# A gated attention and token-mixing kernel: the first loads of x, wv and gate_w issued in another way, and all engines' orders written anew

## The chip, the core and the metric

The kernel runs on one core of one Trainium2 chip. The core has five engines that run at the same time: PE (TensorE, matrix products into PSUM), DVE (VectorE), ACT (ScalarE), POOL (GpSimd) and SP (SyncE, which here only issues DMAs). Sixteen DMA engines move data between HBM and the on-chip memory SBUF; SP and ACT each have a queue for them. The metric is the device time of one execution in microseconds (us), as the median of several runs.

## The reference

x has 2048 rows (tokens) of 448 columns, all in bf16. Two branches are computed from it and mixed by a gate.

```python
g = sigmoid((x * gate_w).sum(-1, keepdims=True))          # one gate per row
a = A(x, wq, wk, wv, wo, beta)
b = B(x, w1, b1, w2, b2)
out = g * a + (1 - g) * b

# A: 16 heads of 28; four segments of 512 rows
q, k, v = x @ wq, x @ wk, x @ wv                          # split into heads and segments
p = softmax(q_s @ k_s.T * 28**-0.5 + mask)                # mask: only keys up to the query, within the segment
a_mem = (phi(q_s) @ M) / (phi(q_s) @ z + 1e-6)            # phi(t) = t + 1 for t > 0, else exp(t)
o_s = sigmoid(beta) * a_mem + (1 - sigmoid(beta)) * (p @ v_s)
M, z = M + phi(k_s).T @ v_s, z + sum(phi(k_s))            # memory of the segments before
A = o @ wo

# B: mixes over the tokens
h = layernorm(x)
u = gelu(h.T @ w1 + b1)                                   # 448 x 1792
B = (u @ w2 + b2).T
```

## The kernel before

**Tiles.** x is held twice: `xh` has 16 tiles of 128 rows (it becomes the layer-normed h in place), and `xT` has the same data transposed, as four overlapping pieces of 128 columns (`C0`) by 2048 rows, in four chunks `tc` of 512 rows. For chunk 0, PE transposes the tiles x0 to x3 with the identity matrix (`trx0_0`, `trx0_1` from x0 and x1, `trx1_0`, `trx1_1` from x2 and x3), and ACT or DVE copies each result from PSUM to `xT` (`xTcp0_00` and so on, lines 695 and 697; the last two digits are the half and the pair of pieces). The other chunks are loaded by transposing DMAs (`dtx1_0` to `dtx3_1`, line 535).

**Projections.** `project` (L711) makes q, k and v: two products of 64 contraction rows each run side by side in the array, so that one step is a pair. `v03` is v of the tiles 0 to 3, with one more column that holds gate_w and gives the gate's sum; `k0`, `q0` are k and q of chunk 0; `k1`, `q1`, `v67` belong to chunk 1. A projection is split into parts: a and b (the first four steps of two outputs each), c and d (the last three). Only `v03` is cut further: `v03s` and `v03t` are the first two steps of a and b, which need two of the three pieces of wv alone (`R_wv[0:2]`), so that they can start before the last piece. The results leave PSUM by `cpv`, `cpk`, `cpq` on ACT or DVE; `gt` takes the tanh of the gate's column on ACT. wk and wq are re-arranged to groups of 32 columns by `padk`, `padx`, `padq` (L655). gate_w comes as rows to `gstage`; PE transposes it (`gtr`) and DVE writes it as the last column of wv (`gw`).

**Attention.** The work has 16 units (4 segments by 4 groups of 4 heads), in 8 pairs. A pair has five steps: `sc` (scores on PE, L973, into the PSUM banks 0 to 3), `exp` (ACT, L982, 128 x 2048) and `mask` (POOL, L985). Each `sc` writes the same four banks, so it waits for the `exp` before it. `pv` is the product with v; `ta`, `rec`, `oa`, `ot` and others finish a unit on DVE. `ek`, `mk`, `phk`, `tk` make phi(k), `mst` and `mem` the memory term. `wo` is the output projection and `ag` its gated evacuation.

**Token mixing.** `bns`, `bna`, `vpe`, `rstd`, `ln` are the layer norm (DVE and POOL). `u` (224 products) and `y` (224, the last tile in two parts) are the two layers on PE; `gsq`, `gvh`, `garg`, `gth`, `gelu` are the gelu on ACT and DVE, `fin` mixes the branches, `out` stores. w1 and w2 come in 15 pieces through three slots (`ldw1_0` to `ldw2_7`). The biases come by `ldb1` and `ldb2`; `btr` on PE turns them into columns.

**Order.** Each engine runs its operations strictly in the order of a list written out in `ORDER` (L308): the names above, with the PSUM banks after "=", and "u1-0:2" for two in a row. An operation that ACT or DVE (or DVE or POOL) can do runs on the engine in whose list it stands. `Sched.plan` reads the lists and `finalize` places a semaphore wait wherever an operation needs another engine's result. An engine that waits holds up everything behind it in its list. The list of SP is the order of its DMA issues.

At the start SP issues x0, then x2 and x3 as one piece, then wv in three pieces, wk and wq in two each; ACT issues x1 and the two pieces of gate_w. POOL makes the identity matrix (`id0`, `id1`, L594 and L595) and clears what must be zero (`z3_0`, `z3_1`, L607, and `v0`, `v1`, L611). PE fills its time with products of no use (`warm`, `fill0` to `fill5`, L640) until x has landed.

Of the kernel before, what the change touches and what calls it, by code (L numbers as in the profile page):

```python
# [5 lines left out]
ACT = mybir.ActivationFunctionType  # L6
# [6 lines left out]
D = 448  # L13
# [288 lines left out]
def pool_cost(n):  # L302
# [7 lines left out]
        warm fill0 fill1 trx0_1=4 trx0_0=5 trx1_1=6 fill2 fill3 gtr fill4 trx1_0=7 fill5 v03s v03a v03t v03b v03c v03d  # L310
        k0a=54 k0b=67 k0c k0d q0a q0b q0d q0c v67a=54 sc0_0 k1a=67 v67c k1c sc0_1 k1b=45 k1d sc0_2 q1a=76 q1b=45 q1c
        q1d sc0_3 u1-0:2=7 u0-0:2=6 u1-2 pv0=4 u1-3 u0-2:3 sc0_4 u0-5:2 u1-4 u0-7 btr=4 u3-0=5 u1-5:3 u3-1 u0-8 u3-2
        u2-0=4 sc1_0 u1-8 u0-9:2 u2-1 u1-9 u2-2:3 u1-10 u2-5:2 u1-11 u0-11 sc1_1 u2-7 u3-3 u0-12 u1-12 u3-4 u1-13:2
        u0-13:2 u2-8 u1-15 u3-5:2 u0-15 u2-9 sc1_2 u2-10 u3-7:3 u4-0:2=7 u2-11:2 u4-2 pv1=6 sc1_3 u3-10 u2-13 u3-11
        u4-3 u5-0:2=6 u4-4 u2-14 u5-2:2 u3-12 u4-5:2 u2-15 u5-4 sc1_4 u3-13:2 u4-7 u5-5 u4-8 u5-6 u7-0=4 u3-15 u5-7
        u7-1:2 u5-8 u4-9 sc2_0 u7-3 u5-9 u4-10 u5-10 u4-11 u5-11:2 u6-0=5 u4-12:3 u6-1 u7-4 u6-2 u4-15 u6-3 sc2_1
        u5-13 u7-5 u6-4 u7-6:3 u5-14:2 pv2=7 sc2_2 u6-5:3 u7-9 u6-8 mst0=7 u7-10 u6-9 pv3=6 u6-10 sc2_3 u7-11:2 u8-0=7
        u7-13:2 u9-0=6 u6-11 u7-15 u8-1:5 u9-1 sc2_4 u6-12 u9-2 u6-13:2 u8-6 u9-3:2 u8-7 u9-5 u6-15 mem4=4 u8-8 u9-6
        u8-9 u9-7:2 sc3_0 u9-9:2 u8-10 pv4=4 u9-11 u8-11 u9-12 u8-12 u9-13 u8-13 u9-14 u8-14 u9-15 u8-15 k2a=54 sc3_1
        k2c k2b=67 k2d sc3_2 q2a=54 q2b=67 q2c q2d sc3_3 v96a=45 v96b=67 v96c v96d sc3_4 u10-0:4=4 pv5=7 u10-4:3  # L320
        mem5=6 mem6=5 u11-0:5=7 sc4_0 u10-7 u11-5:3 u10-8 u11-8 u10-9:2 pv6=5 sc4_1 u13-0=6 u10-11 u11-9:2 u12-0=5
        u10-12 u12-1 u10-13:3 u12-2:3 u11-11 u13-1 u12-5 u11-12:3 u13-2 u11-15 u12-6:2 sc4_2 u12-8 u13-3:3 pv7=4
        mst1=7 u12-9:2 sc4_3 u13-6:2 mem7=7 wo2=4 u13-8 u12-11 u13-9 u12-12 sc4_4 wo0~2=7 u12-13:2 u13-10:4 u12-15
        wo3=4 u13-14:2 wo1=7 sc5_0 k3a=45 k3b=76 k3c k3d sc5_1 v14a=45 pv8=7 v14c pv9=6 wo5=7 mem9=5 sc5_2 q3a=46
        q3b=75 q3c q3d sc5_3 mem8=4 y1-0:2=6 y0-0:2=7 y1-2:2 y3-0:4=4 y1-4:2 sc5_4 y3-4 y0-2:2 y1-6 y0-4 y3-5 y1-7
        y3-6 y0-5 y1-8 y3-7 y1-9:2 sc6_0 y3-8 y0-6 y3-9 y1-11 y0-7 y3-10 y0-8:2 wo4=5 y1-12 sc6_1 y0-10:3 y1-13 wo6=5
        y3-11:3 y0-13 sc6_2 mem11=6 pv10=5 mst2=4 mem10=7 pv11=6 sc6_3 y5-0=5 y2-0=4 y5-1 y2-1 y5-2:2 y2-2 y5-4:2
        y4-0=7 y5-6:2 y4-1:3 sc6_4 y4-4 y6-0=6 y5-8 y6-1 y5-9 y4-5 y2-3 y4-6 y2-4 y4-7 y5-10 y6-2 y4-8 sc7_0 y5-11
        y4-9 y6-3 y4-10:3 y2-5 y4-13 y6-4 y5-12 y2-6 y5-13 y6-5:2 sc7_1 y2-7 wo7=7 y2-8:4 y7-0:2=5 y2-12 y6-7 y2-13
        sc7_2 mem12=7 y7-2:2 pv12=4 y7-4:3 y6-8 mem13=7 sc7_3 y7-7:2 y6-9 y7-9:2 y6-10 y7-11 y6-11:3 wo10=4 y7-12  # L330
        mem14=7 sc7_4 y7-13 pv13=4 wo11=6 wo9=5 wo8=4 y8-0:2=7 y9-0=6 pv14=5 y9-1 pv15=4 y9-2 y8-2 y9-3 y8-3 mem15=5
        y9-4:2 y8-4 y9-6:2 y8-5:3 y9-8 y8-8 y9-9 y11-0:3=5 y9-10 y11-3 y9-11 y11-4 y9-12:2 y10-0=4 y8-9:3 y10-1 y11-5
        y8-12:2 y10-2 y11-6 y10-3 y11-7 y10-4 y11-8 y10-5 y11-9 y10-6:2 y11-10 y10-8 y11-11:2 wo13=6 y10-9:2 wo15=7
        wo14=6 y11-13 wo12=7 y10-11 y13-0:3=6 y15-0:2=5 y14-0=7 y15-2 y14-1 y10-12 y13-3 y15-3:2 y14-2:2 y10-13 y13-4
        y14-4 y15-5 y14-5 y13-5 y15-6 y12-0=4 y14-6 y15-7 y14-7 y13-6 y12-1 y13-7 y14-8:2 y15-8 y12-2 y13-8 y14-10:3
        y15-9 y13-9 y15-10 y12-3 y13-10 y15-11 y12-4:2 y14-13 y13-11:2 y15-12:2 y12-6 y13-13 y12-7:7 y15-0~2=7 y15-1~2
        y15-2~2 y15-3~2 y15-4~2 y15-5~2 y15-6~2 y15-7~2 y15-8~2 y15-9~2 y15-10~2 y15-11~2 y15-12~2 y15-13~2
    """,
    "ACT": """
        ldx1 ldgwb ldgw xTcp0_11 cpv2 gt2 cpv0 cpv1 gt1 gt3 gt0 cpk0_0 ek0_0 cpk0_2 cpk0_3 cpq0_3 cpq0_2 gt4 cpq0_1  # L340
        ek0_1 exp0_0=2 cpv6 gt7 gt6 exp0_1=3 cpk1_3 cpk1_2 exp0_2=4 ek0_2 cpq1_0 cpq1_1 exp0_3=0 cpv5 tb gt5 exp0_4=1
        eq1_1 eq1_0 exp1_0=5 exp1_1=6 eq1_2 gsq1 gsq0 exp1_2=2 ek0_3 gth0 ek1_0 exp1_3=3 gth1 gsq2 exp1_4=0 gth2 gsq3
        exp2_0=1 ek1_1 gth3 gsq4 exp2_1=4 gsq5 gvh5 exp2_2=5 gth5 exp2_3=6 gth4 gsq7 exp2_4=0 gsq6 gth7 ek1_3 exp3_0=2
        gth6 eq1_3 gsq9 gsq8 ek1_2 exp3_1=3 cpk2_1 cpk2_3 cpq2_3 exp3_2=1 cpq2_1 cpv8 gt8 exp3_3=4 cpv9 gt9 cpv11 gt12
        gt11 gt10 exp3_4=7 eq2_1 gth9 ek2_1 exp4_0=0 eq2_0 gth8 exp4_1=5 gsq10 eq2_2 gvh10 ek2_0 gsq11 exp4_2=6 gth10
        exp4_3=2 gth11 ag2 exp4_4=3 gsq12 ag3 gsq13 gvh13 exp5_0=1 cpk3_0 cpk3_3 exp5_1=4 cpv15 gth13 gt15 gt14 eq2_3
        ag5 gth12 exp5_2=7 cpq3_0 ek2_3 exp5_3=0 ek2_2 eq3_2 exp5_4=5 eq3_0 eq3_1 gt13 exp6_0=2 ag4 exp6_1=3 exp6_2=6
        exp6_3=1 exp6_4=4 exp7_0=0 exp7_1=5 ag7 exp7_2=7 eq3_3 exp7_3=2 ag10 exp7_4=3 ag11 ag9 ag8 ag14 ag12
    """,
    "DVE": """  # L350
        xTcp0_00 xTcp0_01 gw bns2 xTcp0_10 bns0 bns1 padk1 bna1 padk0 bns3 bna2 padq0 padq1 bna0 padq3 bna3 padq2 ob0
        cpv3 ln2 ln0 cpk0_1 mk0_0 phk0_0 ln1 bns4 cpv4 bna4 cpq0_0 bns5 bns7 bns6 bna5 bns8 bna6 cpv7 bna7 bns11 bns15
        mk0_1 cpk1_1 cpk1_0 bns9 cpq1_3 bna11 bna15 mo0 bns10 ln4 bna10 ln3 ln5 bns13 ln6 cpq1_2 bna8 ln7 mk0_2 bna9
        bna13 bns12 ta0 bns14 ln9 ln8 bna14 bna12 omgh ln10 rec0 b2c b1c b1h gh mg0 ln11 mq1_0 oc0 phk0_2 mo1 ln12
        ln14 phk0_1 ln13 oc1 oc2 oc3 ln15 mg1 oa0 b1s gvh1 gvh0 phq1_0 garg0 mo2 ta1 gelu0 mk0_3 mg2 gcol0 rec1 garg1
        phk0_3 omg0 b2g0 gelu1 gvh2 mk1_0 garg2 mq1_1 gcol1 phk1_0 gvh3 gelu2 garg3 phq1_1 mo3 gelu3 gvh4 oa1 omg1 ta2
        rec2 mk1_1 garg5 mg3 mq1_2 garg4 msta0 ta3 ot1 gelu5 phk1_1 rec3 ot0 gvh7 mstc0 gelu4 garg7 tm4 oa2 gvh6 garg6
        gelu7 ta4 mk1_3 gelu6 phq1_2 gvh9 gvh8 oa3 garg9 eps4 cpk2_0 rec4 cpk2_2 ot2 phk1_3 mq1_3 om4 mk1_2 cpq2_0
        cpq2_2 phk1_2 garg8 oa4 cpv10 cpv12 ot3 ta5 phq1_3 tm6 tm5 mk2_1 eps6 gelu9 eps5 phk2_1 mq2_1 rec5 ta6 oa5
        gelu8 om5 mq2_0 rec6 ot4 oa6 garg10 gvh11 phq2_0 msta1 ta7 phq2_1 garg11 tm7 mq2_2 mstc1 eps7 gelu10 om6 b2g1  # L360
        gelu11 ag0 ot5 gvh12 rec7 ag1 om7 oa7 garg13 ot6 cpk3_1 cpk3_2 cpq3_3 mk2_0 ot7 ta8 cpv14 ta9 garg12 tm9
        phk2_0 gelu13 gelu12 cpq3_1 cpq3_2 tm8 mk2_3 eps8 phk2_3 mq2_3 rec8 om8 phq2_3 eps9 mk2_2 mq3_2 phk2_2 cpv13
        rec9 om9 mq3_1 gcol2 phq2_2 oa9 omg2 oa8 fin1 ag6 fin3 fin0 tm11 ta10 msta2 tm10 eps11 ta11 eps10 mq3_0 rec11
        b2g2 phq3_2 gcol3 rec10 phq3_1 om10 oa11 ot8 om11 oa10 phq3_0 ot9 fin4 fin5 ot10 mstc2 fin2 tm12 ta12 eps12
        tm13 ot11 rec12 mq3_3 om12 oa12 phq3_3 fin6 fin7 ta13 eps13 tm14 rec13 ot12 oa13 eps14 om13 ta14 rec14 tm15
        ta15 om14 oa14 eps15 ot13 rec15 om15 omg3 oa15 ot14 fin9 b2g3 ot15 fin8 ag13 ag15 fin11 fin10 fin14 fin15
        fin13 fin12 fin15~2
    """,
    "POOL": """
        mhalf v0 id0 z3_1 id1 z3_0 padx1 v1 padx0 vpe0 rstd0 maskg0 vpe4 mask0_0_0 mask0_1_1 rstd4 mask0_1_3 mask0_2_2  # L370
        mask0_2_2~2 vpe8 rstd8 vpe12 rstd12 mask0_4_1 mask1_1_1 mask1_0_0 mask0_4_3 mask0_3_0 wo0 mask1_2_2 mask1_4_1
        mask1_2_2~2 mask2_0_0 mask1_1_3 mask1_3_0 mask2_1_1 mask1_4_3 mask2_2_2 mask2_2_2~2 mask2_3_0 mask2_1_3
        mask3_1_1 mask3_0_0 mask2_4_1 mask3_2_2 mask2_4_3 o4 mask3_3_0 mask3_1_3 mask3_4_1 mask3_2_2~2 o5 mask3_4_3
# [17 lines left out]
def build_kernel(nc, X, WQ, WK, WV, WO, BETA, W1, B1, W2, B2, GW, OUT):  # L391
    NSL, NP = 3, 5
    sch = Sched(nc, {"psum": (4, 5, 6, 7), "p": tuple(range(NP))}, {"p": {}})
    op = sch.op
# [43 lines left out]
    wvx = sb([128, NCT, D + 4])  # L438
# [812 lines left out]
```

## Time and profile before

| | us |
|---|---|
| median of 13 runs | 174.52 (173.71 to 175.99) |
| profiled execution, its own time | 174.22 |
| its span, first to last instruction | 172.5 |
| PE busy (share of the span) | 167.5 (97%) |
| DVE busy | 146.1 (85%) |
| ACT busy | 126.4 (73%) |
| POOL busy | 68.9 (40%) |

The profile is of one execution; its own time is its span and 1.72 us around it. Rows of the profile are groups or merged stretches of instructions: line of the code, engine, operation, what is written and read (all SBUF and PSUM tiles are called t), how often, busy time, and in brackets the idle time before and what ended it. PEld is the weight load that comes before each product. Products are pipelined and their ends are modelled, so that a PE that reads as fully busy need not run at its peak.

### The profile page before, as it was taken

The page shows a single profiled execution, that of the slowest core. Times are in us where ns is not written, and L with a number is a line of the kernel's source. Part 1 is how long each engine was busy: PE and PEld are TensorE (multiplying, and loading weights), DVE is VectorE, ACT ScalarE, POOL GpSimd, SP SyncE. Part 2 cuts the span into 40 slices and gives each one's busy share as a digit, 9 for nine tenths or more (in the row PEclk, how much of TensorE's full clock was granted, in tenths as well). Part 3 has the DMA queues.
Part 4 walks back from the last instruction along what each step waited for, and adds up shares of the span by engine and source line. Part 5 has one row for each costly group of instructions (what it writes and reads, how often), then busy time and mean ns, then how long its engine had stood idle before and what let it go on. Part 6 is the DMA issues. An engine that isn't in the chain of part 4 may idle for free.

```text
span 172.5 us, 4631 instructions
## 1 busy us (share of the span) xinstructions
PE 167.5 (97%) x1900; PEld 81.2 (47%) x1900; DVE 146.1 (85%) x326; ACT 126.4 (73%) x151; POOL 68.9 (40%) x99
## 2 busy tenths in 40 slices
PE   7999999999999999999999999999999999999994
PEld 3444344444445443445554434444644445554552
DVE  0899999879887999998989999998999699885123
ACT  2168999799998999999999989997757876003000
POOL 6250184352355300554270581456428765320000
PEclk9999999999999999999999999999999999999999
DMA  5999999248379459523159340150911878027103
GB/s 151 279 200 274 285 250 257 74 103 241 66 209 145 77 119 307 151 60 72 38 144 292 112 130 0 32 70 12 272 63 55 218 209 260 12 82 211 39 18 106
DMA packets 49749, 24.57 MB, mean 142 GB/s; under 512 B 14256, under 2 KB 49488, under 8 KB 49728
## 3 DMA queue, kind: packets, MB, share of 16 engines
q1 hardware_dynamic: 49576, 24.16, 55.4%
q8 instruction: 15, 0.25, 0.6%
q10 hardware_dynamic: 152, 0.12, 0.2%
q14 instruction: 6, 0.05, 0.1%
HBM read 18.76 MB, written 2.36 MB: 122 GB/s over the span
## 4 chain that ended last, share of the span: by engine, by line
PE 81%; DVE 13%; DMA 3%; SPq 1%; issue 1%
PE t L284 44%; PE t L711 13%; PE t L286 13%; PE t L973 6%; PE t L1011 5%; DMA t<-in_A_wv_dram 3%; DVE t L916 2%; DVE t L749 1%; DVE t L1048 1%; PE t L858 1%; DVE t L761 1%; DVE t L1071 1%; DVE t L1027 1%; DVE t L832 1%; DVE t L1040 1%
## 5 line engine op out<-in xcount | busy, mean ns | idle before, releaser
L284 PE MATMUL t<-t 128*128 128x448 bf16 (+2 forms) x431 | 83.0, 347 | 0.0
L982 ACT ACTIVATE t<-t 128x2048 bf16<-128x2048 f32 x40 | 75.0, 1876 | 8.7 <-PE t L973 8.4
L985 POOL TENSOR_SCALAR_AFFINE_SELECT t<-t 128x512 bf16<-128x512 bf16 x64 | 42.8, 689 | 47.5 <-ACT t L982 46.9
L284 PEld LDWEIGHTS t<-t 128*128 128x128 bf16 x431 | 39.6, 98 | 38.6 <-issue 4.8
L711 PE MATMUL t<-t 64*128 64x512 bf16 (+1 forms) x308 | 35.1, 368 | 1.0 <-DMA t<-in_A_wv_dram 0.4
L286 PE MATMUL t<-t 128*32 128x448 bf16 (+1 forms) x428 | 24.7, 356 | 0.3 <-DVE t L1027 0.2
L1042 POOL TENSOR_TENSOR t<-t 128x448 bf16<-128x448 f32 x12 | 15.5, 1293 | 21.6 <-DVE t L1038 10.3
L711 PEld LDWEIGHTS t<-t 64*128 64x128 bf16 x308 | 15.7, 94 | 17.6 <-PE t L711 1.9
L1118 DVE SCALAR_TENSOR_TENSOR t<-t 128x448 bf16<-128x448 f32 (+2 forms) x17 | 10.7, 645 | 10.1 <-PE t L284 9.9
L1067 ACT ACTIVATE t<-t 128x448 bf16<-128x448 f32 x11 | 7.8, 722 | 14.5 <-PE t L284 14.4
L973 PE MATMUL t<-t 28*128 28x512 bf16 (+3 forms) x256 | 15.8, 301 | 0.1
L286 PEld LDWEIGHTS t<-t 128*32 128x32 bf16 x428 | 10.2, 96 | 8.7 <-issue 2.2
L1027 DVE STREAM_TRANSPOSE t<-t 128x512 f32<-128x512 f32 x16 | 11.3, 705 | 1.9 <-PE t L1011 1.8
L1011 PE MATMUL t<-t 128*32 128x256 bf16 (+3 forms) x256 | 11.9, 300 | 0.3 <-issue 0.3
L973 PEld LDWEIGHTS t<-t 28*128 28x128 bf16 x256 | 4.5, 92 | 14.4 <-issue 4.7
L1048 DVE STREAM_TRANSPOSE t<-t 128x512 bf16<-128x512 bf16 x16 | 11.0, 688 | 0.0
L916 DVE BATCH_NORM_STATS2 t<-t 128x6 f32<-128x448 bf16 x16 | 9.4, 609 | 0.0
L1011 PEld LDWEIGHTS t<-t 128*32 128x32 bf16 x256 | 6.7, 96 | 5.9 <-issue 2.0
L1100 DVE SCALAR_TENSOR_TENSOR t<-t 128x448 bf16<-128x448 f32 x14 | 8.9, 645 | 0.4 <-ACT t L1098 0.4
L1025 DVE STREAM_TRANSPOSE t<-t 128x512 f32<-128x512 f32 x12 | 8.4, 707 | 0.8 <-PE t L284 0.6
L1095 DVE SCALAR_TENSOR_TENSOR t<-t 128x448 f32<-128x448 f32 x14 | 8.9, 636 | 0.0
L1087 ACT ACTIVATE t<-t 128x448 f32<-128x448 f32 x14 | 8.7, 638 | 0.2
(73 smaller groups left out, 165.2 us busy)
## 6 DMA issues: line engine op xcount, KB each, us to landing
t<-in_B_w_dram SPq DMA_DIRECT2D x7, 1024.0 KB, 6.3
t<-in_B_w_dram SPq DMA_DIRECT2D x8, 896.0 KB, 5.3
out_dram<-t SPq DMA_DIRECT2D x15, 112.0 KB, 3.6
t<-in_A_x_dram SPq DMA_DIRECT2D x3, 448.0 KB, 4.6
t<-in_A_wo_dram SPq DMA_DIRECT2D x4, 98.0 KB
t<-in_A_wk_dram SPq DMA_DIRECT2D x1, 336.0 KB, 4.5
t<-in_A_wq_dram SPq DMA_DIRECT2D x1, 336.0 KB, 4.8
spare_heads<-t SPq DMA_DIRECT2D x8, 32.0 KB
```

Of the source, the lines that this page charges most:

```text
L284: return e.matmul(out, w, x, skip_group_check=True, **kw)
L286: last = e.matmul(out[q : q + 32], w[:, q : q + 32], x, skip_group_check=True, **kw)
L711: last = e.matmul(bank(o["b"])[:, 0 : o["n"]], o["w"](r, c), o["x"](r, c), start=first, stop=end, skip_group_check=True)
L916: op("DVE", lambda e: e.bn_stats(st6[:, t, :], xh[:, t, :]), reads=[R_x[t]], writes=[R_st6[t]], name=f"bns{t}", cost=512, prio=P_PROJ - 10)
L973: last = e.matmul(bank(hl)[:, c0 : c0 + w], kT[r, hg, s * 512 + j * 128 : s * 512 + j * 128 + 128], qT[r, hg, s * 512 + 128 * j : s * 512 ...
L982: op("ACT", lambda e: e.activation(pslot(g), ps[:, 0:4, :], ACT.Exp, scale=SCALE), reads=R_bank[0:4], writes=[g.res], take=g, name=f"exp{p ...
L985: op("POOL", lambda e, c0=c0: e.affine_select(pslot(g)[:, :, c0 : c0 + 128], pslot(g)[:, :, c0 : c0 + 128], pattern=[[0, 4], [1, 128]], co ...
L1011: last = e.matmul(bank(cb)[32 * hl : 32 * hl + 32, 128 * j : 512], vaug[:, 4 * s + j, 32 * h : 32 * h + 32], pslot(P_fill[u // 2][f])[:, h ...
L1027: dv(lambda e: e.transpose(t2[:, 0, :], bank(cb)[:, 0:512]), [bres(cb)], [R_tt[tb][0]], "ta", 630, use=(cb,))
L1042: op("POOL", lambda e: e.tensor_tensor(o3, n3[0], n3[1], op=ALU.add), reads=R_tt[tb], writes=[R_ob[tb]], name=f"o{u}", cost=1280, port=Tru ...
L1048: dv(lambda e: e.transpose(oT[:, hg, s * 512 : s * 512 + 512], o), [R_ob[tb]], qres(hg, s), "ot", 635)
L1118: op("DVE", lambda e: e.scalar_tensor_tensor(outst[:, p, c0:c1], bank(b)[:, 0 : c1 - c0], omg[:, T : T + 1], ag(T)[:, c0:c1], op0=ALU.mult ...
```

## The change

Three things are edited.

- The loads. x0 and x1 come as one DMA on SP, x2 and x3 as one on ACT (224 KB each). The first piece of wv (the last 128 rows, 112 KB) stays on SP, and the other two become one DMA of 336 KB on ACT that fills both `R_wv[1]` and `R_wv[2]`. The two pieces of gate_w move from ACT to SP, behind the first piece of wv.
- The lists of all five engines are new. They hold the same operations apart from the loads. Seventeen go to ACT from DVE (xTcp0_00, xTcp0_10, cpv3, cpk0_1, cpk1_1, cpq1_3, gvh1, gvh7, gvh9, cpk2_0, cpq3_3, cpv13, cpv14, ag0, ag1, ag6, ag13), ten from ACT to DVE (cpv0, cpv6, cpk0_2, cpk1_2, gvh5, cpk2_1, gvh10, gvh13, cpv15, ag4), and three from DVE to POOL (padk1, padq2, padq3).
- On SP the load of x4 to x7 comes before the transposing loads of chunk 1, `dtx2_0` takes the early place of `dtx2_1`, and `ldb1` goes behind `ldw1_1`.

The loads, and the heads of the lists:

```diff
-    load_x("SP", 0, 1)
-    load_x("ACT", 1, 1)
-    op("ACT", lambda e: e.dma_start(gstage[0:3, :], GW[0:384].rearrange("(c p) -> c p", p=128)),
+    load_x("SP", 0, 2)
+    load_x("ACT", 2, 2)
+    op("SP", lambda e: e.dma_start(gstage[0:3, :], GW[0:384].rearrange("(c p) -> c p", p=128)),
        writes=[R_gst[0]], name="ldgw", dma=True, prio=-3, cost=450, nbytes=2000)
-    op("ACT", lambda e: e.dma_start(gstage[3:4, :], GW[320:448].rearrange("(c p) -> c p", p=128)),
+    op("SP", lambda e: e.dma_start(gstage[3:4, :], GW[320:448].rearrange("(c p) -> c p", p=128)),
        writes=[R_gst[1]], name="ldgwb", dma=True, prio=-3, cost=450, nbytes=2000)
     op("SP", lambda e: e.dma_start(wvx[:, 3, 0:D], WV[320:448]), writes=[R_wv[0]], name="ldwv0", dma=True, prio=-3,
        cost=450, nbytes=114688)
-    for k, c, n in ((1, 0, 1), (2, 1, 2)):
-        op("SP", lambda e, c=c, n=n: e.dma_start(wvx[:, c : c + n, 0:D],
-                                                 WV[128 * c : 128 * (c + n)].rearrange("(c p) d -> p c d", p=128)),
-           writes=[R_wv[k]], name=f"ldwv{k}", dma=True, prio=-3, cost=450, nbytes=114688 * n)
-    load_x("SP", 2, 2)
+    op("ACT", lambda e: e.dma_start(wvx[:, 0:3, 0:D], WV[0:384].rearrange("(c p) d -> p c d", p=128)),
+       writes=R_wv[1:], name="ldwv1", dma=True, prio=-3, cost=450, nbytes=344064)
...
     "PE": """
-        warm fill0 fill1 trx0_1=4 trx0_0=5 trx1_1=6 fill2 fill3 gtr fill4 trx1_0=7 fill5 v03s v03a v03t v03b v03c v03d
-        k0a=54 k0b=67 k0c k0d q0a q0b q0d q0c v67a=54 sc0_0 k1a=67 v67c k1c sc0_1 k1b=45 k1d sc0_2 q1a=76 q1b=45 q1c
+        warm fill0 trx0_1=4 fill1 trx0_0=5 trx1_1=6 fill2 trx1_0=7 fill3 gtr fill4 fill5 v03t v03s v03a v03b v03c v03d
+        k0a=46 k0b=57 k0c k0d q0b q0a q0d q0c v67a=46 sc0_0 v67c k1a=57 k1c sc0_1 k1b=64 k1d q1a=75 sc0_2 q1c q1b=64
...
     "ACT": """
-        ldx1 ldgwb ldgw xTcp0_11 cpv2 gt2 cpv0 cpv1 gt1 gt3 gt0 cpk0_0 ek0_0 cpk0_2 cpk0_3 cpq0_3 cpq0_2 gt4 cpq0_1
-        ek0_1 exp0_0=2 cpv6 gt7 gt6 exp0_1=3 cpk1_3 cpk1_2 exp0_2=4 ek0_2 cpq1_0 cpq1_1 exp0_3=0 cpv5 tb gt5 exp0_4=1
-        eq1_1 eq1_0 exp1_0=5 exp1_1=6 eq1_2 gsq1 gsq0 exp1_2=2 ek0_3 gth0 ek1_0 exp1_3=3 gth1 gsq2 exp1_4=0 gth2 gsq3
+        ldx2 ldwv1 xTcp0_11 xTcp0_00 xTcp0_10 cpv3 cpv2 gt3 cpv1 gt2 gt0 cpk0_0 gt1 ek0_0 cpk0_1 ek0_1 cpk0_3 cpq0_2
+        gt4 cpq0_1 cpq0_3 exp0_0=2 gt7 gt6 tb cpk1_1 exp0_1=3 cpk1_3 cpq1_3 exp0_2=4 cpq1_0 cpq1_1 exp0_3=0 cpv5 gt5
+        ek0_2 exp0_4=1 eq1_2 exp1_0=5 eq1_1 eq1_0 exp1_1=6 gsq0 gsq1 gvh1 exp1_2=2 gth0 ek0_3 gth1 exp1_3=3 eq1_3 gsq2
...
     "DVE": """
-        xTcp0_00 xTcp0_01 gw bns2 xTcp0_10 bns0 bns1 padk1 bna1 padk0 bns3 bna2 padq0 padq1 bna0 padq3 bna3 padq2 ob0
-        cpv3 ln2 ln0 cpk0_1 mk0_0 phk0_0 ln1 bns4 cpv4 bna4 cpq0_0 bns5 bns7 bns6 bna5 bns8 bna6 cpv7 bna7 bns11 bns15
+        bns0 bns2 xTcp0_01 bna0 gw bns1 bns3 padk0 bna1 bna2 padq1 bna3 padq0 bns6 bns5 cpv0 bns7 bns4 ln0 ln3 bna4
+        mk0_0 bna7 phk0_0 cpk0_2 cpv4 bna6 cpq0_0 bns13 bna5 bns8 bns11 cpv7 cpv6 bns10 bna8 omgh cpk1_0 bns9 ln4 ln1
...
     "POOL": """
-        mhalf v0 id0 z3_1 id1 z3_0 padx1 v1 padx0 vpe0 rstd0 maskg0 vpe4 mask0_0_0 mask0_1_1 rstd4 mask0_1_3 mask0_2_2
+        z3_1 v0 z3_0 id0 v1 id1 padx0 padk1 padx1 vpe0 mhalf padq2 rstd0 padq3 wo0 maskg0 vpe4 mask0_0_0 rstd4
...
     "SP": """
-        ldx0 ldx2 ldwv0 ldwv1 ldwv2 ldwk0 ldwk=0 ldwq0 ldwq=1 ldbeta ldb2 dtx1_0 dtx1_1 ldx4 ldx12 ldb1 ldx8 dtx2_1
-        tk0_0 ldw1_0 ldw1_1 gk0_2 gk0_1 gk0_3 ldw1_2 gq0_2 gq0_1 gq0_0 gk0_0 gq0_3 gk0_h1 gk0_h0 gq0_h1 gq0_h2 gq0_h0
+        ldx0 ldwv0 ldgw ldgwb ldwk=0 ldwk0 ldwq=1 ldwq0 ldx4 dtx1_0 ldbeta dtx1_1 ldx8 ldx12 dtx2_0 tk0_0 ldw1_0 ldb2
+        ldw1_1 ldb1 gk0_1 gk0_3 gk0_2 ldw1_2 gq0_0 gq0_1 gq0_2 gq0_3 ldwo2 gk0_0 gq0_h2 gq0_h1 gk0_h1 gk0_h0 gq0_h0
...
```

## The prediction

> **What bounds the kernel now.** I read the busy time by stretch first (columns: stretch, its length, busy time and count of PE, weight loads, DVE, ACT, POOL, the granted clock, DMA share, GB/s).
>
> ```profile
> 0.00:7.07 7.07, 5.74 (x33) 2.90 (x34) 2.19 (x6) 1.88 (x2) 2.98 (x10) 1.00 0.73 199
> 16.69:30.00 13.31, 12.96 (x155) 5.64 (x156) 13.22 (x42) 12.98 (x17) 6.27 (x10) 1.00 1.03 257
> 30.00:60.00 30.00, 29.69 (x373) 14.14 (x372) 25.98 (x69) 27.75 (x31) 13.32 (x20) 1.00 0.58 132
> 60.00:90.00 30.00, 29.80 (x464) 14.24 (x461) 28.50 (x57) 29.54 (x40) 10.71 (x15) 1.00 0.49 122
> 90.00:120.00 30.00, 29.76 (x273) 13.42 (x269) 29.17 (x60) 27.79 (x33) 14.28 (x18) 1.00 0.42 100
> 120.00:146.00 26.00, 26.00 (x389) 13.21 (x384) 24.33 (x49) 18.84 (x14) 14.79 (x21) 1.00 0.60 171
> ```
>
> After 7.07 PE is never free for long: what delays its first product delays the end, unless a later stall shrinks. But ACT is nearly full too from 16.7 to 120 us (98.06 of 103.31), and DVE from 16.7 to 30. Next the chain of waits: its shares, then its pieces in order (start, length, what).
>
> ```profile
> PE 81%; DVE 13%; DMA 3%; SPq 1%; issue 1%
> ...
> 2.71 4.32 DMA t<-in_A_wv_dram
> 7.07 7.23 PE t L711 x66
> ```
>
> The last piece of wv lands at 2.71 + 4.32 = 7.03 and opens the dense stretch. The timeline has the other steps of the head:
>
> ```profile
> 2.42 0.30 POOL L595 TENSOR_SCALAR_AFFINE_SELECT t<-t 128x128 bf16<-128x128 bf16 x1
> 3.58 1.20 PEld L683 LDWEIGHTS t<-t 128*128 128x128 bf16 x12 [0.50 <-DMA t<-in_A_x_dram]
> 5.09 0.60 ACT L695 ACTIVATE t<-t 128x512 bf16<-128x512 bf16 x1 [1.71 <-PE t L683]
> 9.57 0.54 ACT L830 ACTIVATE t<-t 128x448 bf16<-128x448 f32 x1 [3.89 <-PE t L711]
> 16.69 0.40 PE L973 MATMUL t<-t 28*128 28x512 bf16 x4
> ```
>
> Identity ready at 2.72, first transposes at 3.58 when x has landed, the ACT copy at 5.09, the first evacuation of v at 9.57, the first scores (sc0_0) at 16.69. Of the waits, in us, times, longest:
>
> ```profile
> POOL t L985 <- ACT t L982: 46.9, 20, 9.8
> ACT t L982 <- PE t L973: 8.4, 11, 1.4
> PEld t L973 <- ACT t L982: 4.6, 13, 0.5
> ```
>
> Each scores step needs the exp before it to have left banks 0 to 3, so PE and ACT march together. Transfers of x take this from issue to landing:
>
> ```profile
> DMA to landing us min/median/max: 2.5/2.7/2.8
> ```
>
> **What the skill says.** "DMA: Bandwidth & Descriptors", section "Issuing engines are not separate DMA queues": DMAs of SP and ACT run on the same 16 engines; a second issuer saves only issue time. The trace agrees so far: two 112 KB pieces on two queues landed together at 3.3 and 3.5. "TensorE: Matmul & The Clock Gate", Part 1: a free-running window of about 3.4 us decides whether the array runs at half clock. Here 512-column warm-up products start 0.42 us apart, later ones 0.21, though the granted clock reads 1.00 throughout. "GPSIMD Engine Reference", section 4.1: one-input operations run at roughly line rate; its 3.1 measures about 2.6 cycles an element for two-input ones. The 512-element select in this trace takes 0.64 us, 1.25 ns an element.
>
> **The head, part by part.** Names are mapped to rows in order (each engine has as many rows as its list has names).
>
> x: the four tiles go out at 0.80 and 0.81 as two 224 KB pieces. Before, all 448 KB had landed at 1.26 + 2.8 = 4.06, the first two tiles at 3.3 and 3.5. I take 4.0 for both halves: the first half later, the second no earlier.
>
> Identity: the new POOL list puts z3_1, v0, z3_0, id0, v1 ahead of id1. The rows 0.96 + 0.53 + 0.95 + 0.25 + 0.53 + 0.30 = 3.52, less about 0.06 overlap each, from 0.80: ready at 4.0 (2.72 before). With x at 4.0 this costs nothing more; were x at 3.5 it would be the bound.
>
> PE: a group of four transposes takes 0.43 (12 weight loads in 1.20 to 1.29), a fill 0.21. From 4.1: trx0_1, fill1, trx0_0, trx1_1 end near 5.6. ACT now makes three of the four copies (11, 00, 10) at some 0.55 each: 5.65 to 7.3. The first v product, v03t, needs the third; behind it in PE's list stand all of v, k0 and q0, and every evacuation on ACT and DVE waits for those. So v starts near 7.3, and from its first step: 14 steps of 0.195 end at 10.05. Before, two steps were done before 7.07 and 12 were left: 9.4. That is **+0.6**.
>
> wv: one 336 KB piece on ACT, 112 KB on SP. If the two queues share evenly, up to 224 KB of wk goes along before its last byte: from 4.0, 672 KB (688,000 bytes) at the page's 279 GB/s is 2.5 us, so 6.5, under 7.3. A straggling engine as late as 7.0 is still covered; uncovered, each 0.1 us counts in full. The v03s/v03t cut, which let two steps run on two of three pieces, is worth nothing now.
>
> gate_w: two issues (0.54 and 0.25) move from ACT to SP ahead of wk; SP loses one x issue and two of wv (about 1.3), so wk is issued near 2.65, not 3.18. Gate rows land by about 4.7, gtr runs near 6.2: nothing.
>
> SP's later order: x4 ahead of the transposed loads, dtx2_0 (2.4 us of issue, if like dtx1_0) in place of dtx2_1. ldw1_0 goes out about 1.2 us later than 15.88. It landed at 22.2 and is used at 25.7: hidden, with 2 us to spare. ldb1 now follows ldw1_1 and lands near 27, btr comes near 29: hidden.
>
> POOL takes padk1, padq2, padq3. padq2 has 1344 elements: 1.35 us at line rate, 1.7 at the select's rate, 3.5 at 2.6 ns (what padx0's 0.52 against padx1's 0.23 gives for 112 elements more). I take 1.7: bna3 waits for wq until 9.5, then vpe0, padq2, rstd0 (1.05), padq3 end at 13.3; q0b would come at 13.05. The 0.25 is covered by DVE, next.
>
> DVE up to cpq0_0, which sc0_0 needs: x4 lands about 10.7 (wq near 9.2, then 448 KB at 279 GB/s); from there bns6 to cpq0_0 are 15 rows, 7.25 less 0.85 of overlap: 17.1. So sc0_0 is at 17.1, **+0.4**: part of the 0.6 is absorbed, since DVE set this point before too.
>
> ACT from then on: seventeen operations come to it, ten leave. Two copies fall in its idle time before 9.6 (1.0 us). Of the rest, up to the second unit pair, only gvh1 (0.6) is net; cpv3, cpk0_1, cpk1_1, cpq1_3 come and cpv0, cpv6, cpk0_2, cpk1_2 go. ACT's first evacuation is 0.6 later too; so exp1_x would be 1.2 later, less about 0.3 of idle time there (its finish minus its summed work grows from 10.3 to 10.7 by exp1_4): +0.9. PE waits for each exp and has no later slack, so the end takes it: **+0.9** in place of the 0.4. Later net extras (about 1.4 us by exp6_0) meet ACT's 2.2 idle us between 90 and 120: nothing.
>
> PE's list has the same 608 names; weighted by their rows' durations the forty scores steps keep their places, most within 0.6 us, none moved by over 1.8; runs of one array mode are 113 before, 110 after; the tail (2.35) has the same last steps. So the rest of the reordering counts nothing. Sum: the profiled execution's 174.22 + 0.9 = 175.1; it lies 0.30 under the median 174.52, so **175.4**.
>
> **Rivals.**
> Faster: DVE relief. DVE's list is about 5 us shorter, and 2 to 3 us shorter up to gelu2. PE's larger pauses after 14 us (0.35, 0.34, 0.46, 0.69, 0.34, 0.38, 0.42) sum to 3.0, several ended by DVE. If two thirds go (-2.0) and the head costs +0.6: -1.4, so 173.1. It decides the sign once the pauses shrink by more than the 0.9 above. Against it: work leaves DVE for ACT, which is as full.
> Slower still: padq2 at 3.5 us puts padq3 at 15.1, q0b 2.05 late; or PE idle from 3.2 to 4.1 leaves the half clock on for one more window, seven v steps at double time (about 1.4 on top of 0.6). Either gives about +2.2: 176.7. The first counts from about 1.7 us on, where its cover by DVE ends.
> No change: ACT's idle time swallows its extra work and DVE leads as before: 174.5.
> The two large transfers landing x well ahead of 4.0 would help little: identity at 4.0 holds.
>
> **Numbers.** Likeliest 0.45 at 175.4, its own range 174.8 to 176.2; slower still 0.20; no change 0.14; faster 0.21. A measurement here tells about 0.5% (0.87 us) from no change. Of the likeliest, some 0.29 lies above 175.39: slower 0.49; within 0.16 + 0.14 = 0.30; faster 0.21. The range 173.0 to 176.9 holds both outer cases' centres.
>
> **What would show it.** Right: identity near 4.0; ACT rows of L695 three times, the last ending near 7.3 and releasing v, not wv; sc0_0 near 17.1; exp1 rows 0.9 later; PE's busy total unchanged. Wrong: v starting by 6.7; pauses of PE after 20 us falling by over 1 us; padq2 at 3 us; products at half speed after 7 us.

## The result and the profile after

The changed kernel takes 176.40 us (median of 11 runs, 175.41 to 176.78), the kernel before 174.17 over all its 48 runs beside it: a ratio of 1.0124, 95% interval 1.0103 to 1.0146, so 2.2 us slower. Ratios here and below are worked out from the fast runs of both kernels in one session, those within 1.5% of the kernel's fastest, so they differ a little from the quotients of the medians. The profiled execution took 176.63 with a span of 174.88; before, 174.22 and 172.50. The spans differ by 2.38 us. Code lines after the loads stand three lower than before (L711 is now L708, L973 is L970).

The page of the changed kernel, busy time and count by engine, then the shares of the chain that ended last:

```profile
PE 168.8 (97%) x1954; PEld 82.0 (47%) x1954; DVE 143.3 (82%) x316; ACT 129.8 (74%) x158; POOL 71.5 (41%) x102
...
PE 92%; DVE 2%; POOL 2%; issue 1%; ACT 1%; POOLq 0%
```

DVE is relieved (146.1 to 143.3) and ACT takes more (126.4 to 129.8), and yet the chain is now more PE than before (92% for 81%). The same stretches as shown of before, with the same columns:

```profile
0.00:7.07 7.07, 5.50 (x28) 3.00 (x28) 1.91 (x6) 2.60 (x4) 3.67 (x12) 1.00 0.74 237
16.69:30.00 13.31, 12.99 (x162) 5.23 (x162) 12.31 (x35) 12.87 (x20) 5.73 (x9) 1.00 0.99 222
30.00:60.00 30.00, 28.94 (x373) 13.93 (x374) 25.68 (x69) 28.29 (x31) 12.31 (x17) 1.00 0.56 146
```

From 16.69 to 30 us PE is as full as before, with DVE 0.9 us less busy: the relief of DVE did not make PE fuller there. From 30 to 60 it is 0.75 us less busy than before (29.69), which is a pause that comes up again below. That points to the head for most of the loss. The timeline of the head of the changed kernel (start, length, engine, line, what, count, in brackets the idle time before and what ended it):

```profile
3.63 0.30 POOL L592 TENSOR_SCALAR_AFFINE_SELECT t<-t 128x128 bf16<-128x128 bf16 x1
4.07 0.58 PE L680 MATMUL t<-t 128*128 128x128 bf16 x4 [0.73 <-POOL t L592]
5.76 1.57 ACT L692 ACTIVATE t<-t 128x512 bf16<-128x512 bf16 x3 [2.62 <-PE t L680]
7.39 10.89 PE L708 MATMUL t<-t 64*128 64x449 bf16 x92 [0.16 <-ACT t L692]
9.24 0.15 PEld L708 LDWEIGHTS t<-t 64*128 64x128 bf16 x2 [0.23 <-issue]
9.62 0.15 PEld L708 LDWEIGHTS t<-t 64*128 64x128 bf16 x2 [0.23 <-issue]
9.99 7.85 PEld L708 LDWEIGHTS t<-t 64*128 64x128 bf16 x76 [0.23 <-PE t L708]
```

Identity, transposes, three ACT copies and the start of v stand where the prediction had them. Then comes what it did not have in its likeliest case. The weight loads of v's steps begin 0.375 us apart (9.24, 9.62, 9.99), where before they were about 0.19 apart: the array runs at half rate until 10 us, and only then do the loads close up into one stretch. Its granted clock reads 1.00 all the while, as the windows above show. Seven of v's 14 steps are slow. Its last step begins at 11.21 (9.18 before), the first scores at 18.41 (16.69), and the last product of PE ends at 172.49 (170.11).

### The profile page after: what moved, and what is told of

It reads as the page before. It is cut to its first block, busy times and chain, and to the rows that moved or that the text cites. A ratio compares the mean times of both kernels' runs of the same rounds, so it can differ in the third digit from the quotient of the medians.

```text
span 174.9 us, 4745 instructions
## 1 busy us (share of the span) xinstructions
PE 168.8 (97%) x1954; PEld 82.0 (47%) x1954; DVE 143.3 (82%) x316; ACT 129.8 (74%) x158; POOL 71.5 (41%) x102
## 4 chain that ended last, share of the span: by engine, by line
PE 92%; DVE 2%; POOL 2%; issue 1%; ACT 1%; POOLq 0%
PE t L284 45%; PE t L708 20%; PE t L286 14%; PE t L970 7%; PE t L1008 5%; POOL t L604 1%; ACT t L692 1%; PE t L680 1%; DVE t L1024 1%; PE t L855 1%; DVE t L1115 1%; POOL t L608 0%; DVE t L746 0%; DVE t L1037 0%; DVE t L1034 0%
## 5 line engine op out<-in xcount | busy, mean ns | idle before, releaser
L284 PE MATMUL t<-t 128*128 128x448 bf16 (+3 forms) x413 | 79.8, 347 | 0.4 <-DVE t L1034 0.3
L982 POOL TENSOR_SCALAR_AFFINE_SELECT t<-t 128x512 bf16<-128x512 bf16 x64 | 45.5, 728 | 58.7 <-ACT t L979 58.1
L284 PEld LDWEIGHTS t<-t 128*128 128x128 bf16 x413 | 38.0, 98 | 37.6 <-issue 4.6
L708 PE MATMUL t<-t 64*128 64x512 bf16 (+1 forms) x308 | 36.2, 378 | 0.5 <-ACT t L692 0.2
L286 PE MATMUL t<-t 128*32 128x448 bf16 (+1 forms) x500 | 27.5, 354 | 0.0
L708 PEld LDWEIGHTS t<-t 64*128 64x128 bf16 x308 | 15.9, 97 | 18.2 <-PE t L708 2.9
L1064 ACT ACTIVATE t<-t 128x448 bf16<-128x448 f32 x14 | 10.0, 726 | 13.7 <-PE t L284 12.8
L1039 POOL TENSOR_TENSOR t<-t 128x448 bf16<-128x448 f32 x12 | 14.1, 1176 | 13.9 <-DVE t L1035 9.6
L286 PEld LDWEIGHTS t<-t 128*32 128x32 bf16 x500 | 12.1, 96 | 9.8 <-issue 2.2
L970 PE MATMUL t<-t 28*128 28x512 bf16 (+3 forms) x256 | 15.8, 301 | 0.1
L1024 DVE STREAM_TRANSPOSE t<-t 128x512 f32<-128x512 f32 x16 | 11.2, 707 | 1.3 <-PE t L1008 1.3
L1008 PE MATMUL t<-t 128*32 128x512 bf16 (+3 forms) x256 | 11.3, 300 | 0.0
L1045 DVE STREAM_TRANSPOSE t<-t 128x512 bf16<-128x512 bf16 x16 | 10.9, 688 | 0.4 <-POOL t L1039 0.3
L970 PEld LDWEIGHTS t<-t 28*128 28x128 bf16 x256 | 4.5, 92 | 14.0 <-ACT t L979 5.1
L1090 DVE TENSOR_SCALAR t<-t 128x448 f32<-128x448 f32 x11 | 7.3, 676 | 2.2 <-ACT t L1084 2.1
L1008 PEld LDWEIGHTS t<-t 128*32 128x32 bf16 x256 | 6.5, 96 | 5.4 <-issue 0.6
```

The lines of the kernel that those rows point to most:

```text
L284: return e.matmul(out, w, x, skip_group_check=True, **kw)
L286: last = e.matmul(out[q : q + 32], w[:, q : q + 32], x, skip_group_check=True, **kw)
L708: last = e.matmul(bank(o["b"])[:, 0 : o["n"]], o["w"](r, c), o["x"](r, c), start=first, stop=end, skip_group_check=True)
L970: last = e.matmul(bank(hl)[:, c0 : c0 + w], kT[r, hg, s * 512 + j * 128 : s * 512 + j * 128 + 128], qT[r, hg, s * 512 + 128 * j : s * 512 ...
L982: op("POOL", lambda e, c0=c0: e.affine_select(pslot(g)[:, :, c0 : c0 + 128], pslot(g)[:, :, c0 : c0 + 128], pattern=[[0, 4], [1, 128]], co ...
L1008: last = e.matmul(bank(cb)[32 * hl : 32 * hl + 32, 128 * j : 512], vaug[:, 4 * s + j, 32 * h : 32 * h + 32], pslot(P_fill[u // 2][f])[:, h ...
```

## The experiments

Theory: the pause of PE from 3.34 to 4.07 keeps the array at half rate into v, which costs about 1.3 us; the later start of v costs 0.4 more; the loads themselves cost nothing. Rivals: the lists cost the 2.2 us by ACT's extra work or by PE's own order; the late identity costs it; the new loads cost it.

**More and fewer products before the transposes.** In the changed kernel, and the other way round in the kernel before:

```diff
-    warm_up(5, "warm", -1)
+    warm_up(7, "warm", -1)      # a1_warm7, on the changed kernel
+    warm_up(3, "warm", -1)      # b1_warm3, on the kernel before
```

> The changed kernel with 7 warm-up products instead of 5, so PE has work until about 4.0 us, when the first transposes can start. Half-clock theory: the array reaches full rate before v, the v steps are 0.19 us apart from the first on (they were 0.375 apart from 7.39 to 9.99), and the time falls by 1.0 to 1.3 us, from 176.4 to about 175.2. Rival (the new lists cost the time, the half clock is a matter of the execution): v steps still 0.375 apart until about 10 us in the profile, time within 0.3 us of 176.4.

> The kernel before with 3 warm-up products instead of 5, so PE is idle for about 1 us before x lands, as in the changed kernel. Half-clock theory: full rate comes one window later, the first v steps are 0.375 us apart, time up by 0.8 to 1.4 us, from 174.2 to about 175.3. Rival: v steps 0.19 apart, time within 0.3 us of 174.2.

With seven, 175.23 us (16 runs), 1.0070 [1.0046, 1.0095] of before: 1.17 us less than the changed kernel by the medians, 0.9 us by the two ratios, whose intervals do not touch. Its timeline:

```profile
5.73 0.63 PE L680 MATMUL t<-t 128*128 128x128 bf16 x4
6.16 0.31 PE L637 MATMUL t<-const-bfloat16-1.0 128*128 128x256 bf16 x1
7.39 9.56 PE L708 MATMUL t<-t 64*128 64x449 bf16 x92 [0.48 <-ACT t L692]
17.07 0.40 PE L970 MATMUL t<-t 28*128 28x512 bf16 x4
```

v begins at 7.39 as in the changed kernel, but 92 products take 9.56 us for 10.89. The first scores come 1.34 earlier, at 17.07.

The other direction failed. With three, the kernel before took 174.42 (22 runs), 1.0005 [0.9985, 1.0024]: no change. The half rate did last longer there (to 7.8 us), and four v steps were slow, but two of those fall before 7.07, when v had to wait for wv anyway. The first scores came 0.39 later, and a pause of 0.69 us at 54.9 was absent from this profile. A half rate costs only the part of it that lies over work on the path.

**Small products in the gap.** To fill the gap without moving the large products:

```diff
     warm_up(5, "warm", -1)
+    warm_up(16, "tiny", -1, 0.0, 64)
...
-        warm fill0 trx0_1=4 ...
+        warm tiny fill0 trx0_1=4 ...
```

> The changed kernel with 16 small warm-up products (64 columns) added after the 5 large ones, so that PE is busy until about 4 us and its program is 32 instructions longer at the head. Half-clock theory: v steps 0.19 us apart, time about 1 us under the change, near 175.3. If the 1.06 us pause within the first memory product is the program's refill reaching PE late, the refill comes some 32 instructions earlier in the work, the pause shrinks by more than 0.5 us, and the time falls below the version with 7 large warm-up products (175.2), to about 174.7. If the pause has another cause: it stays at 0.9 to 1.1 us, time as that version.

174.81 us (22 runs), 1.0031 [1.0018, 1.0045]. All v steps take 0.19. So 1.6 us of the 2.2 us go without a change to any load or to any order behind the head. The time is the one expected from a shorter pause inside `mst0`, but that pause was not shorter: 1.5 us from start to start, 1.25 in the changed kernel. Its profile gains on that of a1_warm7 only near 124 us, where it lacks a stop that comes up below. The runs also lie closer together: their standard deviation is 0.26 us, that of the changed kernel 0.41. (Its profiled execution, at 175.39, is one of its slowest; there PE waited 0.31 us for the transposing load of x at 13.5 and the first scores came at 17.53.)

**The loads alone, and the lists alone.**

```diff
# b2_loads_only: the kernel before with the change's loads; its lists only take their names
-        ldx1 ldgwb ldgw xTcp0_11 ...
+        ldx2 ldwv1 xTcp0_11 ...
-        ldx0 ldx2 ldwv0 ldwv1 ldwv2 ldwk0 ldwk=0 ...
+        ldx0 ldwv0 ldgw ldgwb ldwk0 ldwk=0 ...
# a3_loads_back: the changed kernel with the loads of before, the reverse of the above
```

> The kernel before with its own lists, only the loads of x, wv and gate_w as in the change. If the loads themselves cost time (the first x tiles land later): transposes start at 3.8 instead of 3.58, time up by 0.2 to 0.6 us. If the new lists carry the cost: wv lands at 5.8 instead of 7.0, v runs without a stop from about 6.4, and the time is 0.2 to 0.6 us under the kernel before, about 173.8.

> The changed lists with the loads of the kernel before. If the lists carry the whole cost: identity still at 3.9, v again from about 7.4, part of it at half clock, and 1.0 to 1.5% over the kernel before, like the whole change. If the loads carry it: within 0.5% of the kernel before.

The loads alone: 173.63 us (14 runs), 0.9975 [0.9949, 1.0001]; no loss, rather a small gain. v begins at 6.22 and never stops for wv, so its last step starts at 8.71 (9.18 before), and the first scores at 16.22. The lists alone: 176.15 us (6 runs), 1.0107 [1.0067, 1.0146], hardly less than the whole change. **The whole loss is the lists'.**

**The late identity.** In the kernel before, POOL's clears go ahead of the identity, as the changed list has them:

```diff
-        mhalf v0 id0 z3_1 id1 z3_0 padx1 v1 padx0 ...
+        mhalf z3_1 v0 z3_0 id0 v1 id1 padx1 padx0 ...
```

> The kernel before with only POOL's first clears moved ahead of the identity matrix. Identity near 4.0, transposes from 4.1 instead of 3.58. Identity theory: the transposed copies end 0.5 later, near 7.2, with PE idle from 3.4 to 4.1; v's last step ends 0.2 to 0.5 later, or about 1 us later if the half clock stays on: +0.2 to +1.0 us. Prediction's view (identity costs nothing): within 0.2 us of the kernel before.

174.05 us (14 runs), 1.0001 [0.9970, 1.0033]. The transposes start at 4.12 instead of 3.61, after a pause of 0.56, and yet the full rate came at 5.1 us and v at 6.24. In the kernel before, the late identity costs nothing by itself. In the changed kernel it is what the transposes wait for; an early identity there was not measured.

**Copies of transposed x back on DVE.**

```diff
# ACT
-        ldx2 ldwv1 xTcp0_11 xTcp0_00 xTcp0_10 cpv3 ...
+        ldx2 ldwv1 xTcp0_11 cpv3 ...
# DVE
-        bns0 bns2 xTcp0_01 bna0 gw ...
+        xTcp0_01 xTcp0_00 xTcp0_10 gw bns0 bns2 bna0 ...
```

> The changed kernel with two of the three ACT copies of the transposed x back on DVE, ahead of the first layer-norm statistics. If the third copy sets the start of v: v starts near 6.7 instead of 7.39. With the half clock still on until about 10 us that start buys about half of it, 0.3 to 0.4 us, so about 176.0; if the start counted in full, 0.6 us, so 175.8. If the start of v doesn't matter (DVE sets the first scores): 176.4, or more because the statistics come later.

175.71 us (6 runs), 1.0096 [1.0058, 1.0133], not told apart from the changed kernel. v begins at 7.16 (7.39), and the half rate lasts to 8.7 in its profile. Half of 8.7 - 7.16 is 0.77 us; without it the first scores would be at 17.63 - 0.77 = 16.86, 0.2 us ahead of a1_warm7. That would be the worth of the third copy on ACT, an estimate from this one profile.

**gate_w first.** A version that might beat both, from the loads-only kernel:

```diff
-        ldx0 ldwv0 ldgw ldgwb ldwk0 ...
+        ldx0 ldgwb ldgw ldwv0 ldwk0 ...
```

> The kernel before with the new loads, but gate_w ahead of the first piece of wv on SP, so that its transpose no longer holds up the last transposes of x: v starts when wv lands, near 5.9 instead of 6.2. If each step at the head is carried to the end: 0.2 to 0.4 us under the kernel with the new loads alone (173.6), 0.4 to 0.8 us under the kernel before. If DVE sets the first scores anyway: as that one, 0.4 under the kernel before.

173.41 us (22 runs), 0.9969 [0.9951, 0.9987]: the lowest median of all, 0.3% under the kernel before, but not told apart from the loads alone (0.9975 [0.9949, 1.0001]). The chain of waits in its head (start, length, what):

```profile
0.81 2.87 DMA t<-in_A_x_dram
...
3.72 1.34 PE t L680 x12
...
5.94 7.56 PE t L708 x70
```

The wait for wv that opened the dense stretch of the kernel before (7.07) is gone: x, transposes, v follow one another, and v runs from 5.9.

**Another place for every product in the instruction stream.** The pause of PE between 30 and 60 us stands in the chain of the changed kernel here:

```profile
55.14 0.44 PE t L855 x57
55.58 1.06 issue
56.64 0.22 PE t L855 x7
```

L855 is `mst0`, 64 products of 32 columns. All five profiles of versions with the new lists and transposing loads stop in it, for 0.78 to 1.5 us from start to start, each after the same number of products from the kernel's beginning (596 of about 1954), even where 16 were added ahead. The kernel before has its pause of 0.69 us behind product 597, just past its `mst0`. The DMA records show 15 packets of 16 KB marked as instructions in each run (16 in d2_plain_shift60). The Trainium skill, "Vector Engine (DVE) Microarchitecture Reference", section 2.1, gives every instruction 64 bytes; PE's 3908 loads and products would be 250 KB, and the 15 packets are 246 KB. That suggests that PE's instructions are fetched in pieces of 256 and that the short products of `mst0` outrun a piece. I tried to move the place, in versions whose transposing transfers are plain copies:

```diff
# all four: dma_start_transpose(...) becomes dma_start(...) of as many bytes
# d1_plain_warm7: warm_up(7, "warm", -1)
# d2_plain_shift60:
-    warm_up(5, "warm", -1)
+    warm_up(2, "warm", -1)
+    warm_up(63, "tiny", -1, 0.0, 32)
# d3_plain_warm7_dve: seven, and the copies on DVE as in a4_copies_dve
```

> The changed kernel with its 18 transposing transfers (x for the later tokens, and the features of k) made plain copies of as many bytes: the two transpositions are left out, so it stands only as the base of the three versions that follow, which leave out the same. All theories expect the changed kernel's head (v from 7.4, last v step after 10, first scores at about 18) and its pause of about 1 us in mst0; the time is within 1 us of 176.4 unless the plain copies land so much earlier that a wait on them goes.

> The base with plain copies, with seven warm-up products instead of five. Half-clock theory: all 14 v steps take 0.19, the first scores start 1.0 to 1.4 earlier than in the base, and the time is 0.9 to 1.3 less. The pause in mst0 stays (0.7 to 1.3 us).

> The base with plain copies, its five warm-up products of 512 columns taken apart into two of 512 and 63 of 32 columns: the array should be busy about as long as with five to six of the large ones, but every later product has a place 60 further back in TensorE's instruction stream. Theory of the instruction fetch: the pause inside mst0 belongs to place 597 of the product stream (it stood there in all five profiled versions with the new lists, 0.78 to 1.5 us), because instructions are fetched in packets of 16 KB and the 64 short products of mst0 use them up in half a microsecond. Moved back by 60, mst0 begins after place 597, whose neighbours are then longer products; the pause leaves mst0, and from the first scores to 57 us the kernel gains 0.5 to 1.2 us on the base with seven warm-up products. Rival, a wait in the lists themselves (bank 7, or the features of k late): the pause stays in mst0 and nothing is gained. If the short products leave the half clock or run past the transposes, the head shows it, and the part after the first scores is compared alone.

> The base with plain copies, seven warm-up products, and two of the three copies of transposed x back on DVE (xTcp0_01, xTcp0_00, xTcp0_10 ahead of gw and the statistics) as in the kernel before. If the two head terms add (half clock, and 0.2 for the third copy on ACT): v starts at 7.15, its last step at 9.65, the first scores 0.2 earlier than with seven warm-up products alone, and the time is 0.2 to 0.5 less than there. If the DVE lists cannot afford the copies, the later statistics move the first scores back, and the time is no less than there.

| | us (runs) | ratio to before | v starts | first scores |
|---|---|---|---|---|
| d0_plain | 175.36 (20) | 1.0069 [1.0044, 1.0094] | 7.38 | 17.12 |
| d1_plain_warm7 | 175.22 (16) | 1.0053 [1.0028, 1.0077] | 6.67 | 16.36 |
| d2_plain_shift60 | 174.48 (12) | 1.0025 [0.9995, 1.0056] | 6.69 | 17.10 |
| d3_plain_warm7_dve | 175.34 (18) | 1.0062 [1.0043, 1.0081] | 6.95 | 17.36 |

The test of the place came to nothing in `mst0`, because the base has no pause there any more. The timeline of d0_plain:

```profile
53.68 0.67 PE L857 MATMUL t<-t 128*32 128x32 bf16 x64
54.25 0.73 PE L1010 MATMUL t<-t 128*32 128x512 bf16 x16
```

All 64 run through. The instruction packet before it began at 51.1 there, 2.6 us ahead of `mst0`; in the changed kernel it began at 54.2, 0.7 us ahead. So the pause needs more than the place: it needs a late packet. The six profiles that stop at this place (the five, and the kernel before) go on 2.40 to 2.72 us after the packet began, whether the stop is 0.69 or 1.5 us; d0_plain gets there 3.1 us after it and does not stop.

The same shows near 124 us. In seven of the nine profiles with the new lists PE stands there before one product, and goes on 2.27 to 2.43 us after a packet of instructions began (3.09 in a3_loads_back). With two more warm-up products (a1_warm7 against the changed kernel, d1 and d3 against d0) it stands two products earlier in the work, so the stop keeps its place in the instruction stream. a5_tiny and d2_plain_shift60, with 16 and 60 products more, have no packet between 117 and 125.8 us and no such stop. That is where d2_plain_shift60 gains: it has its first scores where the base has them (PE waited for x and for ACT at 12.9 and 17.1), is still level with it at 124 us, and ends 0.55 earlier. So the stops follow the place and the packets. That PE waits for its instructions fits all of this and is not shown directly, and why a packet begins late stays open.

Two more expectations of these four failed. Seven warm-up products gave 0.14 us here and not 0.9 to 1.3, with intervals that overlap: the profile of d0_plain has the same gap as the changed kernel, but the half rate ended at 7.5 us in it, so only its first v step was slow. In the profiles the first scores of d1_plain_warm7 still come 0.76 earlier, and it keeps that lead to 120 us; 0.54 of it goes at the stop near 124 us. And the copies on DVE gained nothing on top: PE waited 0.6 us at the first scores for a copy on ACT (L807).

**When the full rate comes.** Read in each profile from the starts of consecutive equal products (0.83 ns a column at half rate, 0.42 at full rate):

| profiled execution | PE pause before the transposes | full rate from |
|---|---|---|
| before | 0.05 | 5.1 to 5.6 |
| b2_loads_only, b4_gate_first | 0.2 | 3.9 at the latest, 4.8 |
| d2_plain_shift60 | 0.33 | 4.15 |
| b3_ident_late | 0.56 | 5.1 |
| a1_warm7, a5_tiny, d3_plain_warm7_dve | none | 6.2 to 6.6 |
| d1_plain_warm7 | none | 4.1 at the latest |
| d0_plain, a3_loads_back, a4_copies_dve, after | 0.72 to 0.73 | 7.5, 8.2, 8.7, 10.1 |
| b1_warm3 | 0.84 | 7.8 |

The nine with a pause of 0.56 us or less have the full rate by 6.6 us, the five with 0.72 or more from 7.5 to 10.1. The Trainium skill, "TensorE: Matmul & The Clock Gate", Part 1, says that one busy window of about 3.4 us turns the rate up and that the windows run free of the kernel's start. If the window must lie wholly behind the pause, one that begins at 4.07 or later ends between 7.5 and 10.9, and b1_warm3's between 7.0 and 10.4. All five lie in there. Without such a pause the window counts from 0.83, which makes 4.2 to 7.7; seven of the nine fit to 0.1 us, but d1_plain_warm7 (by 4.1) and b2_loads_only (by 3.9) are too early for it. b3_ident_late at 5.1, 1.0 us behind its pause, shows that a pause of 0.56 us need not be left out of the window. No run set the window's phase, so the windows are the page's account, with which these numbers agree in the main. Each row is one execution.

## Why the prediction was off by 1 us

Said was +0.9 us, 175.4 from 174.52; measured is +2.2, 176.40 from 174.17. The direction was right, and the time lies in the wide range but above the likeliest case.

**Right.** x landed at 3.79 and 4.06 (said: 4.0), the identity at 3.93 (4.0), wv by 5.8 (6.5, and covered as said), the third ACT copy at 7.33 (7.3), and v began at 7.39 (7.3), released by that copy and not by wv. gate_w cost nothing. The later pieces of w1 cost no wait of PE: the first landed at 24.98, and the products that use it run from 27.4.

**The step that failed** is "from its first step: 14 steps of 0.195 end at 10.05". Seven of them took 0.375, and v's last step began at 11.21 instead of 9.9. a1_warm7, which changes only the rate, has its last step at 9.88 and its first scores at 17.07, where the prediction said 17.1; its time is 175.23 where the prediction said 175.4 (1.2 over the kernel before of its session, said 0.9). The missed term is therefore 1.2 us by the medians (176.40 - 175.23), 0.9 by the ratios and 1.34 in the profiles. It was in the text, as the second branch of the rival "slower still", with the right count of steps and the right size, at 176.7; only its chance (0.20 for both branches together) was low for it. Two entries could have raised it. The list moves fill1 from ahead of the first transposes to behind them, so that the products without use end at 3.34 instead of 3.56, while the identity comes 1.2 us later. And a window that starts anywhere after 4.07 ends at 9.2 on average, an estimate from that page's 3.4 us: half of 9.2 - 7.39 is 0.9 us, to be expected on average over the executions, where the prediction had 1.4 in at most one of five.

**Right in sum, by luck.** The prediction put +0.9 on ACT's extra work, carried to the end. With the rate repaired (a1_warm7) the exps of pair 1 start 0.42 to 0.66 later than before, not 0.9, and that is PE's later head (0.38 at the first scores), with little of ACT's. At 50 to 53 us exp2_1 and exp2_2 are even 0.1 to 0.3 earlier than before; the end is 0.79 later, and the 0.41 that this is more than the head's 0.38 comes behind that point. So a growing lag of ACT was not the carrier. The first scores at 17.1 came out right, but not by the reason given, that x4 lands at 10.7 (10.8 by its own figures) and DVE is busy from there on: in a1_warm7 x4 is in by 9.55, and DVE then stands for 0.27 us until 13.93, when ACT has done `ek0_0`. The scores follow the copies cpq0_0 (DVE) and cpq0_1 (ACT) by about 0.15 us, in a1_warm7 (these end at 16.93 and 16.91) and in the changed kernel, here:

```profile
17.57 0.69 DVE L803 CAST t<-t 128x512 bf16<-128x512 f32 x1
17.64 0.59 ACT L805 ACTIVATE t<-t 128x512 bf16<-128x512 f32 x1
18.37 0.13 PEld L970 LDWEIGHTS t<-t 28*128 28x128 bf16 x4 [0.54 <-ACT t L805]
```

Both copies need products of PE, and so move with its head; which of the two ends the wait is not told apart.

**Too large.** padq2 took 1.30 us, below the taken 1.7 and just under the lower bound 1.35; padq3 ended at 12.06, not 13.3. 1344 elements in 1.30 us is 0.97 ns each, so the copy was faster than the select (1.25) from which the 1.7 was worked out.

**Too small.** "The rest of the reordering counts nothing": it counted 0.66 in the profiled executions. The sum of the 2.38 us of the spans' difference is 1.34 (rate; changed kernel less a1_warm7 at the first scores) + 0.38 (later head; a1_warm7 less before there) + 0.41 (a1_warm7 behind the first scores) + 0.25 (what the changed kernel loses more than a1_warm7 there). The 0.25 comes as 0.16 in `mst0` (1.25 us from start to start, 1.08 in a1_warm7; the kernel before has 0.69 just behind its `mst0`) and the rest mostly near 93 us. The other stop is near 124 us, where the chain of the changed kernel names DVE:

```profile
123.15 0.58 DVE t L1115
...
123.75 1.30 DVE t L1024 x2
125.06 0.32 DVE t L1033
...
125.40 0.36 DVE t L1034
...
125.79 3.01 PE t L284 x15
```

There `y5-0` starts 0.66 us after `mem10`, the product before it. But `y5-0` needs only its PSUM bank, which L1024 frees at 125.05, and not the reciprocal that L1034 makes; and a1_warm7 stands about as long two products earlier, with no wait at all (0.43 us, before the last of four scores products). The two profiles are 1.57 us apart ahead of this place and 1.59 behind it, so it is part of the 0.41 and not of the 0.25.

**The rivals.** Faster by DVE's relief did not happen: DVE's busy time fell by 2.8 us, but PE's in the stretches shown fell too, by 0.72 (42.65 to 41.93), where fewer pauses would have raised it. The first branch of "slower still", a slow padq2, is excluded by its 1.30 us. Of "no change" one half came true: ACT's extra work was not carried to the end. It fell by the later head.

## What to carry to other kernels

Count the time between the last filler product and the first real one as a cost of its own: 0.7 us of idle PE at the start left the array at half rate for up to six more us, 1.2 us of time, and sixteen products of 64 columns in that gap took it away. The size varies: with plain copies for the transposing loads, filling the same gap gave 0.14 us. When a list or a load moves what the first products wait for, move the fillers with it. Undoing one part at a time also showed that the new loads cost nothing and may gain 0.2% (0.3% with gate_w first, with an interval wholly below 1), which the new lists hid: they cost 1%.

## What was not expected of the hardware

- The granted clock in the trace reads 1.00 where products run at half rate; only the distance of their starts tells (0.375 us for a step of 449 columns, then 0.195).
- Much the same head has the full rate at different times: d0_plain, a3_loads_back and the changed kernel pause alike, and it came at 7.5, 8.2 and 10.1 us. The two versions with small products in the gap have the smallest standard deviations, 0.26 us (a5_tiny) and 0.28 (d2_plain_shift60), but a4_copies_dve, which has the gap, comes near with 0.34, so the spread is not shown to be the gap's.
- Between two kernels with the same lists a delay is carried unchanged nearly everywhere: from 18.41 to 52 us the changed kernel runs 1.33 us behind a1_warm7. It changes at the stop in `mst0` (to 1.49) and in other pairs at the one near 124 us: a3_loads_back has its first scores 0.52 us ahead of the changed kernel, is 0.91 ahead at 120 us, and ends 0.06 behind it.
- PE can stop for about 1 us inside a burst of short products with no semaphore to wait for (`mst0`), in five profiles at the same place of its instruction stream, and goes on 2.4 to 2.7 us after a 16 KB packet marked as instructions began. The chain can lay such a stop to another engine: the one near 124 us is put down to DVE.
